# Four transformer layers on one core: own LayerNorm chains for the first four token tiles, a one-step norm, another token order, later loads of the feed-forward weights

## The chip, the cores and the metric

The kernel runs on one core of one Trainium2 chip. A core has five engines with queues of their own: PE (TensorE, matrix products), ACT (ScalarE), DVE (VectorE), POOL (GpSimd) and SP (SyncE, which here only issues DMAs). They meet through semaphores alone; each executes its queue in order. The metric is the device time of one execution in microseconds (us), as the median of several runs. Beside the times stands one profiled execution, from which all the durations come.

## What is computed

x has 2048 tokens of 512 elements, bf16. Two layers alternate, A, B, A, B, each with a LayerNorm ahead and a residual sum behind:

```python
x = x + A(layernorm(x))      # linear attention, 32 heads of 16
x = x + B(layernorm(x))      # relu(x @ w1) @ w2, 512 -> 1376 -> 512

# A:  q, k, v = x @ wqkv;  phi(t) = where(t > 0, t + 1, exp(t)) + 1e-6
kv  = einsum("bhsd,bhse->bhde", phi(k), v)      # a sum over all tokens
z   = einsum("bhsd->bhd", phi(k))
o   = einsum("bhqd,bhde->bhqe", phi(q), kv) / (einsum("bhqd,bhd->bhq", phi(q), z) + 1e-6)
return o @ wo
```

Tokens meet only in the sums kv and z, and these do not depend on the order of the tokens.

## The kernel before

**Tiles and stages.** The tokens are cut into 16 tiles of 128 (one token per partition) and 4 chunks of 4 tiles. For each tile: statistics, norm (`xn`), transposition (`Tb`, features on partitions). Layer A then takes, in its pass `p1` over chunks, the K projection of each tile (`a_k`, four matmuls of 512 columns) and the Q projection of each chunk (`a_q`, four groups of four matmuls). Each projection is evacuated from PSUM by `phi_evac` (L489): two passes of ACT (linear, exp) and two of DVE. `a_z` and `a_g` sum z and G = xn^T phi(K); V is never projected for each token, since kv = G Wv is made once from G (`a_kv`), masked to the heads (KVT, L569), multiplied by wo (`a_m`) and copied to `Mf` (L576). `a_fin` applies Mf to the scaled phi(Q). Between these, `a_den` makes the denominators and `a_pqs` (matmuls of `rdc`, "rdx") scales phi(Q) by them. `bar` is that middle stage. Layer B is `b_h` (w1, relu) and `b_out` (w2, residual).

**What sets the order.** The kernel first lists all operations with what they read and write, with a duration assumed for each, and `_list_schedule` (L118) then fixes every engine's queue: the earliest start wins within a window of the listed operations. Operations given as `add_flex` may go to one of several engines, by the assumed durations. PSUM has 8 banks, handed out in the same pass. So a changed duration or dependence reorders queues far behind it.

**First loads.** SP issues, in this order (L364 to L384): tile 0 of x (`ld_x0a`), tiles 1 to 3, the K and the Q columns of wqkv, chunks 1, 2 and 3 of x, the V columns, wo, w1, and w2 in two parts. Tile n holds the tokens 128 n to 128 n + 127, so that in DRAM a partition's row of one tile is 1 KB, and the four rows of a chunk lie 128 KB apart.

**First statistics.** `ln_stats_first` (L426) is bn_stats and bn_aggr on DVE, giving mean and variance (`mv`). Then `veps` (DVE), the power -0.5 on POOL (`rstd`), `nbias` = -mean * rstd (DVE), and the norm xn = x * rstd + nbias. Tile 0 has a chain of its own (L713 to L725), tiles 1 to 3 share one (L726 to L737). Chunks 0 and 1 are transposed on PE (`transpose_pe`, L472, evacuated by ACT or DVE, L485 and L486), chunks 2 and 3 by DMA transposes (L467) on SP. The first of these waits for all the weight loads (`ALL_LOADS`, L386, L751).

**Warm-up.** 16 matmuls of zeros (L399) run on PE while the first loads come.

Of the kernel before, what the change touches and what calls it, by code (L numbers as in the profile page):

```python
# [7 lines left out]
ALU = alu_op_type.AluOpType  # L8
ACTF = mybir.ActivationFunctionType
# [22 lines left out]
C_DVE_NORM_BF = 325.0  # L32
C_POOL_POW = 1000.0
C_POOL_NORM = 900.0
C_SP_ISSUE = 60.0
# [209 lines left out]
def build_kernel(nc, A_x, A_wqkv, A_wo, B_w1, B_w2, out, n_layers_pairs=2, K_STT=0, Q_STT=0, A_PE_CHUNKS=1, windows=None,  # L245
                 WARM=16, SPLIT0=True, TAIL_SPLIT=True, LAST_HALVES=True, FIRST_PE_CHUNKS=2,
                 flex_strict=True, flex_bias_dve=0.0):
# [18 lines left out]
    with es:  # L266
# [39 lines left out]
        nhalf = sb("nhalf", [128, 4], F32)  # L306
        veps0 = sb("veps0", [128, 1], F32)
        rstd0 = sb("rstd0", [128, 1], F32)
        nbias0 = sb("nbias0", [128, 1], F32)
        wrm = sb("wrm", [128, 512], BF16)  # L310
# [52 lines left out]

        x_v = A_x[0].rearrange("(n p) d -> p n d", p=128)  # L364
        out_v = out[0].rearrange("(n p) d -> p n d", p=128)
        def ld_x(t, lo=0):
            dma(lambda e, t=t: e.dma_start(xin[:, 4 * t + lo:4 * t + 4, :], x_v[:, 4 * t + lo:4 * t + 4, :]),
                [], [("xin", i) for i in range(4 * t + lo, 4 * t + 4)], 1500.0 * (4 - lo) / 4.0, "ld_x%d" % t)
        dma(lambda e: e.dma_start(xin[:, 0, :], x_v[:, 0, :]), [], [("xin", 0)], 450.0, "ld_x0a")
        wq_v = A_wqkv.rearrange("(c p) n -> p c n", p=128)  # L370
        ld_x(0, 1)
        dma(lambda e: e.dma_start(wqkv[:, :, D:2 * D], wq_v[:, :, D:2 * D]), [], [("wk",)], 1500.0, "ld_wk")  # L372
        dma(lambda e: e.dma_start(wqkv[:, :, 0:D], wq_v[:, :, 0:D]), [], [("wq",)], 1500.0, "ld_wq")  # L373
        for t in range(1, NCH):
# [4 lines left out]

        dma(lambda e: e.dma_start(w1[:], B_w1.rearrange("(c p) n -> p c n", p=128)), [], [("w1",)], 4000.0, "ld_w1")  # L380
        dma(lambda e: e.dma_start(w2[:, 0:nfull, :], B_w2[0:nfull * 128, :].rearrange("(c p) n -> p c n", p=128)),
            [], [("w2a",)], 3800.0, "ld_w2a")
        if FLAST < 128:
            dma(lambda e: e.dma_start(w2[0:FLAST, NFC - 1, :], B_w2[nfull * 128:DFF, :]), [], [("w2b",)], 600.0, "ld_w2b")  # L384
        W2KEYS = [("w2a",), ("w2b",)] if FLAST < 128 else [("w2a",)]
        ALL_LOADS = [("wk",), ("wv",), ("wq",), ("wo",), ("w1",)] + W2KEYS  # L386

# [5 lines left out]
        if WARM > 0:  # L393
            wt = alloc_bank()

            def _warm(e):
                last = None
                for k in range(WARM):
                    last = e.matmul(psv[:, wt, :], wrm[:, 0:128], wrm[:, :], start=True, stop=True)  # L399
                return last  # L400
            g.add(PE, _warm, [("wrm",)], [("ps", wt)], WARM * 400.0, name="warm")
        g.add(POOL, lambda e: e.memset(onesf[:], 1.0), [], [("onesf",)], 200, name="ms_ones")
# [22 lines left out]

        def ln_stats_first(i):  # L426
            g.add(DVE, lambda e: e.bn_stats(bst[:, i, :], xin[:, i, :]), [("xin", i)], [("bst", i)], C_DVE_BNST, name="bnst%d" % i)  # L427
            g.add(DVE, lambda e: e.bn_aggr(mv[:, i, :], bst[:, i, :]), [("bst", i)], [("mean", i), ("var", i)], C_DVE_SMALL, name="bnag%d" % i)
# [269 lines left out]
        def store_chunk(t):  # L698
            if t == NCH - 1 and TAIL_SPLIT:
# [9 lines left out]
                [("xin", i) for i in range(4 * t, 4 * t + 4)] + [("T", i) for i in range(NT)], [("out", t)], 1500.0, "st%d" % t)  # L709

        def ln_first(t):
            if t == 0 and SPLIT0:
                ln_stats_first(0)  # L713
                g.add(DVE, lambda e: e.tensor_scalar(veps0[:, :], mv[:, 0, 1:2], 0.0, EPS, ALU.max, ALU.add),
                      [("var", 0)], [("veps0",)], C_DVE_SMALL, name="veps0a")
                g.add(POOL, lambda e: e.tensor_tensor(rstd0[:, :], veps0[:, :], nhalf[:, 0:1], ALU.pow),
                      [("veps0",), ("nhalf",)], [("rstd0",)], C_POOL_POW, name="rstd0a")
                g.add(DVE, lambda e: e.scalar_tensor_tensor(nbias0[:, :], mv[:, 0, 0:1], -1.0, rstd0[:, :], ALU.mult, ALU.mult),
                      [("mean", 0), ("rstd0",)], [("nbias0",)], C_DVE_SMALL, name="nbias0a")
                g.add_flex([(DVE, lambda e: e.tensor_scalar(xn[:, 0, :], xin[:, 0, :], rstd0[:, 0:1], nbias0[:, 0:1], ALU.mult, ALU.add),  # L720
                             C_DVE_NORM_BF),
                            (ACT, lambda e: e.activation(xn[:, 0, :], xin[:, 0, :], ACTF.Identity, scale=rstd0[:, 0:1],
                                                         bias=nbias0[:, 0:1]), C_ACT_SB_AP)],
                           [("xin", 0), ("rstd0",), ("nbias0",)], [("xn", 0)], name="norm0a")
                transpose_pe(0)  # L725
                for i in range(1, 4):  # L726
                    ln_stats_first(i)
                sl = slice(1, 4)
                g.add(DVE, lambda e: e.tensor_scalar(veps[:, sl], mv[:, sl, 1], 0.0, EPS, ALU.max, ALU.add),
                      [("var", i) for i in range(1, 4)], [("veps", 0)], C_DVE_SMALL, name="veps0b")  # L730
                g.add(POOL, lambda e: e.tensor_tensor(rstd[:, sl], veps[:, sl], nhalf[:, 0:3], ALU.pow),
                      [("veps", 0), ("nhalf",)], [("rstd", 0)], C_POOL_POW, name="rstd0b")
                g.add(DVE, lambda e: e.scalar_tensor_tensor(nbias[:, sl], mv[:, sl, 0], -1.0, rstd[:, sl], ALU.mult, ALU.mult),
                      [("mean", i) for i in range(1, 4)] + [("rstd", 0)], [("nbias", 0)], C_DVE_SMALL, name="nbias0b")
                for i in range(1, 4):
                    ln_norm(i, True)
                    transpose_pe(i)  # L737
                return
            for i in range(4 * t, 4 * t + 4):
                ln_stats_first(i)  # L740
            ln_chunk(t, True)
            for i in range(4 * t, 4 * t + 4):
                ln_norm(i, True)
                if t < FIRST_PE_CHUNKS:
                    transpose_pe(i)
            if t >= FIRST_PE_CHUNKS:
                tr_dma(t)
# [18 lines left out]
        def layer_steps(layer):  # L766
# [3 lines left out]
            if layer % 2 == 0:  # L770
# [4 lines left out]
                def p1(t):  # L775
                    if first_layer and t + 1 < NCH:
                        ln_first(t + 1)
                    for i in range(4 * t, 4 * t + 4):
                        a_k(i)
# [194 lines left out]
```

## Time and profile before

| what | value |
|---|---|
| median of 3 runs | 294.8 us (293.8 to 294.86) |
| the profiled execution | 295.03 us, of which span 293.3 us |
| PE busy | 283.8 us (97%) |
| ACT busy | 170.3 us (58%) |
| DVE busy | 158.1 us (54%) |
| POOL busy | 33.1 us (11%) |
| DMA, mean over the span | 57 GB/s |
| granted TensorE clock | 1.0 |

The span runs from the first to the last instruction of the program; what is left of the execution's time lies around it. The page of the profile has the busy time of each engine, the span cut into 40 slices (a digit for each, in tenths), the chain of work that ended last, the costliest groups of instructions and the DMA issues. The chain is followed back from the last instruction, at each step to what released it; where it names a DMA or another engine, the engine that waited stood still. In the timeline each line has start, duration, engine, source line, operation, what is written and read, and in brackets how long the engine was idle before and who released it. PEld is the load of matmul weights, and SPq is SP issuing a DMA.

### The profile page before, as it was taken

Reading aid. Unit: us, or ns where it says so; the run is one execution under the profiler, and the core shown is the slowest. Engines: PE = TensorE matmul, PEld = TensorE weight load, DVE = VectorE, ACT = ScalarE, POOL = GpSimd, SP = SyncE. Lnnn points to the kernel's source line nnn. Section 1 sums busy time; section 2 is a strip of 40 time slices with the busy share of each in tenths; the row PEclk is TensorE's granted clock in tenths of the full one; section 3 lists DMA queues with packets and bytes.
Section 4 is the critical chain, followed back from the end, with each engine's and each line's share of the span. In section 5 each row is a group of like instructions: output and inputs, shape, how many; then the busy total and the mean of one; then the engine's idle time right before and its main releaser. Section 6 shows DMA issues by size and latency. Waiting matters only on the chain.

```text
span 293.3 us, 4232 instructions
## 1 busy us (share of the span) xinstructions
PE 283.8 (97%) x1610; PEld 133.5 (46%) x1636; DVE 158.1 (54%) x443; ACT 170.3 (58%) x351; POOL 33.1 (11%) x43
## 2 busy tenths in 40 slices
PE   7699999989999999999999999999999999999996
PEld 3345444434454454454444444444445445454444
DVE  5699774999720293361454748928973037020122
ACT  2798496687765365397434999248786505407000
POOL 4012100002410040020020300000241002000000
PEclk9999999999999999999999999999999999999999
DMA  7991330000260016031003300000026003303022
GB/s 221 356 370 41 64 54 0 2 0 0 52 130 0 2 35 126 1 71 21 0 2 72 70 4 0 0 2 0 1 58 124 0 2 91 72 2 89 0 74 72
DMA packets 37796, 16.72 MB, mean 57 GB/s; under 512 B 29616, under 2 KB 37264, under 8 KB 37776
## 3 DMA queue, kind: packets, MB, share of 16 engines
q1 hardware_dynamic: 37776, 16.45, 22.8%
q8 instruction: 13, 0.21, 0.3%
q14 instruction: 7, 0.06, 0.1%
HBM read 7.01 MB, written 2.10 MB: 31 GB/s over the span
## 4 chain that ended last, share of the span: by engine, by line
PE 88%; DVE 6%; DMA 3%; ACT 2%; issue 1%; SPq 1%
PE ps L510 87%; DMA xin<-in_A_x_dram 3%; DVE big L606 2%; DVE xn L459 1%; DVE xres L521 1%; ACT Mf L576 1%; ACT big L493 1%; PE ps L481 0%; DVE bst L427 0%; DVE big L503 0%; DVE emscr L497 0%; ACT sqscr L527 0%; SPq L373 0%; ACT escr L495 0%; SPq L372 0%
## 5 line engine op out<-in xcount | busy, mean ns | idle before, releaser
L510 PE MATMUL ps<-w,big 128*128 128x512 bf16 (+3 forms) x355 | 76.0, 372 | 0.4
L510 PE MATMUL ps<-Tb,w 128*128 128x512 bf16 x320 | 70.4, 379 | 0.0
L510 PEld LDWEIGHTS ps<-w,big 128*128 128x128 bf16 (+1 forms) x363 | 35.3, 98 | 40.4
L527 ACT ACTIVATE sqscr<-xres 128x512 bf16<-128x512 f32 x48 | 30.0, 628 | 40.1 <-DVE xres L521 39.6
L655 ACT ACTIVATE big<-ps 128x512 bf16<-128x512 f32 x70 | 41.6, 598 | 17.9 <-PE ps L510 17.9
L510 PEld LDWEIGHTS ps<-Tb,w 128*128 128x128 bf16 x320 | 30.8, 98 | 35.9
L493 ACT ACTIVATE big<-ps 128x512 bf16<-128x512 f32 x64 | 41.2, 648 | 9.0 <-PE ps L510 8.8
L521 DVE SCALAR_TENSOR_TENSOR xres<-ps,xres 128x512 f32<-128x512 f32 x32 | 21.9, 689 | 38.2 <-PE ps L510 38.0
L495 ACT ACTIVATE escr<-ps 128x512 bf16<-128x512 f32 x64 | 41.6, 667 | 0.4 <-DVE emscr L497 0.4
L447 POOL TENSOR_TENSOR rstd<-veps,nhalf 128x4 f32<-128x4 f32 x15 | 16.1, 1070 | 204.5 <-DVE veps L445 183.3
L518 DVE TENSOR_TENSOR xin<-ps,xres 128x512 bf16<-128x512 f32 x15 | 10.4, 692 | 46.6 <-PE ps L510 46.6
L510 PE MATMUL ps<-wqkv,Tb 128*128 128x512 bf16 x122 | 28.6, 379 | 2.7 <-DVE Tb L486 1.2
L510 PE MATMUL ps<-Tb,wqkv 128*128 128x512 bf16 x128 | 30.6, 379 | 0.0
L510 PE MATMUL ps<-Mf,big 128*128 128x512 bf16 x122 | 29.0, 380 | 1.3 <-ACT Mf L576 0.8
L510 PE MATMUL ps<-big,xn 128*128 128x512 bf16 x124 | 29.7, 379 | 0.3
L497 DVE TENSOR_SCALAR emscr<-escr 128x512 bf16<-128x512 bf16 x64 | 18.4, 296 | 18.5 <-ACT escr L495 18.4
L503 DVE TENSOR_TENSOR big<-big,emscr 128x512 bf16<-128x512 bf16 x64 | 26.4, 421 | 1.2
L606 DVE TENSOR_TENSOR big<-big,ps 128x512 bf16<-128x512 bf16 x32 | 19.9, 680 | 1.3 <-PE ps L510 1.3
L510 PEld LDWEIGHTS ps<-wqkv,Tb 128*128 128x128 bf16 x128 | 12.1, 98 | 17.2 <-DVE Tb L486 1.7
L510 PEld LDWEIGHTS ps<-Mf,big 128*128 128x128 bf16 x128 | 11.9, 98 | 16.2 <-ACT Mf L576 1.3
L510 PEld LDWEIGHTS ps<-big,xn 128*128 128x128 bf16 x128 | 11.5, 97 | 13.1 <-issue 1.5
L510 PEld LDWEIGHTS ps<-Tb,wqkv 128*128 128x128 bf16 x128 | 11.5, 97 | 12.3 <-DVE big L606 0.4
(74 smaller groups left out, 196.2 us busy)
## 6 DMA issues: line engine op xcount, KB each, us to landing
wqkv<-in_A_wqkv_dram SPq DMA_DIRECT2D x3, 512.0 KB, 7.1
xin<-in_A_x_dram SPq DMA_DIRECT2D x3, 512.0 KB, 9.1
out_dram<-xin SPq DMA_DIRECT2D x3, 512.0 KB, 2.9
w<-in_B_w_dram SPq DMA_DIRECT2D x1, 1376.0 KB, 11.0
w<-in_B_w_dram SPq DMA_DIRECT2D x1, 1280.0 KB, 12.8
wo<-in_A_wo_dram SPq DMA_DIRECT2D x1, 512.0 KB, 9.4
xin<-in_A_x_dram SPq DMA_DIRECT2D x1, 384.0 KB, 3.2
out_dram<-xin SPq DMA_DIRECT2D x1, 256.0 KB, 2.1
```

What stands on the lines that cost most here:

```text
L447: g.add(POOL, lambda e: e.tensor_tensor(rstd[:, sl], veps[:, sl], nhalf[:, 0:4], ALU.pow), [("veps", t), ("nhalf",)], [("rstd", t)], C_POO ...
L459: (DVE, lambda e: e.tensor_scalar(xn[:, i, :], src, rstd[:, i:i + 1], nbias[:, i:i + 1], ALU.mult, ALU.add), C_DVE_NORM_BF if first else 4 ...
L493: g.add(ACT, lambda e: e.activation(dst_ap, psv[:, b, :], ACTF.Identity, bias=1.0 + 1e-6, scale=1.0), [("ps", b)], [dst_key], C_ACT_PSUM, ...
L495: g.add(ACT, lambda e: e.activation(escr[:, s, :], psv[:, b, :], ACTF.Exp), [("ps", b)], [("escr", s)], C_ACT_EXP, name=name + "_exp")
L497: g.add(DVE, lambda e: e.tensor_scalar(emscr[:, s, :], escr[:, s, :], 1.0, 1e-6, ALU.min, ALU.add), [("escr", s)], [("emscr", s)], C_DVE_B ...
L503: g.add(DVE, lambda e: e.tensor_tensor(dst_ap, dst_ap, emscr[:, s, :], ALU.max), [dst_key, ("emscr", s)], [dst_key], 340.0, name=name + "_ ...
L510: last = e.matmul(o, l, r, start=st, stop=sp, skip_group_check=skip)
L518: g.add(DVE, lambda e: e.tensor_tensor(xin[:, i, :], psv[:, b, :], src, ALU.add), [("ps", b), skey], [("xin", i)], C_DVE_PSUM, name="resid ...
L521: g.add(DVE, lambda e: e.scalar_tensor_tensor(xres[:, i, :], psv[:, b, :], 0.0, src, ALU.add, ALU.add, accum_out=s1[:, i:i + 1]), [("ps", ...
L527: g.add(ACT, lambda e: e.activation(sqscr[:, q, :], xres[:, i, :], ACTF.Square, accum_out=s2[:, i:i + 1]), [("xres", i)], [("sqscr", q), ( ...
L606: g.add(DVE, lambda e, j=j, u=u: e.tensor_tensor(unit_ap(u), unit_ap(u), psv[:, bs[j], :], ALU.mult), [("ps", bs[j]), ("big", u)], [("big" ...
L655: g.add_flex([(ACT, lambda e, M=M, b=b, u=u: e.activation(unit_ap(u, M), psv[0:M, b, :], ACTF.Relu), C_ACT_PSUM), (DVE, lambda e, M=M, b=b ...
```

## The change

- Each of tiles 0, 1, 2 gets its own chain: bn_stats, bn_aggr, `veps`, a one-column power on POOL, norm. The statistics of tile 2 wait until tile 0 is normed and tile 1's `veps` is done. Tile 3's mean and mean square are summed by two passes of ACT, and its variance and `veps` are made by POOL.
- The norm of these four tiles is one step, (x - mean) * rstd, on DVE alone; `nbias` and the choice between ACT and DVE are gone for them.
- Tokens are dealt the other way: partition p holds the tokens 16 p to 16 p + 15, one for each tile, in the input and the output. A partition's row of a chunk is 4 KB on end, with 16 KB from partition to partition.
- w1 and w2 are loaded after the DMA transposes of chunks 2 and 3 (`ld_ff`), and the first DMA transpose no longer waits for them.
- The warm-up has 13 matmuls instead of 16. Some assumed durations are changed, of x and weight loads and of the warm-up.

```diff
-                 WARM=16, SPLIT0=True, ...
+                 WARM=13, SPLIT0=True, ...
-        x_v = A_x[0].rearrange("(n p) d -> p n d", p=128)
-        out_v = out[0].rearrange("(n p) d -> p n d", p=128)
+        x_v = A_x[0].rearrange("(p n) d -> p n d", p=128)
+        out_v = out[0].rearrange("(p n) d -> p n d", p=128)
...
+        def ld_ff():
+            after = [("T", i) for i in range(4 * FIRST_PE_CHUNKS, NT)]
+            dma(... w1 ..., after, [("w1",)], 4000.0, "ld_w1")
+            dma(... w2 ..., after, [("w2a",)], 3800.0, "ld_w2a")
+            if FLAST < 128:
+                dma(... w2 ..., after, [("w2b",)], 600.0, "ld_w2b")
-        ALL_LOADS = [("wk",), ("wv",), ("wq",), ("wo",), ("w1",)] + W2KEYS
+        ALL_LOADS = [("wk",), ("wv",), ("wq",), ("wo",)]
...
+        def ln_own(i):
+            mu = mv[:, i, 0:1] if i < 3 else mean[:, i:i + 1]
+            g.add(POOL, lambda e: e.tensor_tensor(rstd[:, i:i + 1], veps[:, i:i + 1], nhalf[:, 0:1], ALU.pow),
+                  [("veps1", i), ("nhalf",)], [("rstd1", i)], C_POOL_POW1, name="rstd_%d" % i)
+            g.add(DVE, lambda e: e.tensor_scalar(xn[:, i, :], xin[:, i, :], mu, rstd[:, i:i + 1], ALU.subtract, ALU.mult),
+                  [("xin", i), ("mean", i), ("rstd1", i)], [("xn", i)], C_DVE_NORM_BF, name="norm%d" % i)
+            transpose_pe(i)
...
             if t == 0 and SPLIT0:
+                for i in range(3):
+                    ln_stats_first(i, [("xn", 0), ("veps1", 1)] if i == 2 else [])
+                    g.add(DVE, ... veps[:, i:i + 1] <- mv[:, i, 1:2] ..., C_DVE_TINY, name="veps_%d" % i)
+                    ln_own(i)
+                g.add(ACT, lambda e: e.activation(sqscr[:, 0, :], xin[:, 3, :], ACTF.Identity, scale=INV_D, accum_out=mean[:, 3:4]), ...)
+                g.add(ACT, lambda e: e.activation(sqscr[:, 1, :], xin[:, 3, :], ACTF.Square, scale=INV_D ** 0.5, accum_out=s2[:, 3:4]), ...)
+                g.add(POOL, ... nm2[:, 3:4] <- mean * mean ..., name="nm2_3")
+                g.add(POOL, ... var[:, 3:4] <- s2 - nm2 ..., name="var_3")
+                g.add(POOL, ... veps[:, 3:4] <- max(var, 0) + EPS ..., name="veps_3")
+                ln_own(3)
                 return
...
                     if first_layer and t + 1 < NCH:
                         ln_first(t + 1)
+                        if t + 2 == NCH:
+                            ld_ff()
```

## The prediction

> **What bounds the kernel now.** First the page's busy line and its 40 slices.
>
> ```profile
> span 293.3 us, 4232 instructions
> PE 283.8 (97%) x1610; PEld 133.5 (46%) x1636; DVE 158.1 (54%) x443; ACT 170.3 (58%) x351; POOL 33.1 (11%) x43
> ...
> PE   7699999989999999999999999999999999999996
> ```
>
> TensorE (PE) is the bound: 283.8 of 293.3 us, and its digit is below 9 only in the first two slices, once near 60 us and in the last. Only there can this change gain or lose. Of 9.5 us not busy, 1.25 stand ahead of the first warm-up matmul and about 2 behind the last matmul. So I read the chain that ended last, in order of time, for what the first slices wait on.
>
> ```profile
> 2.78 8.10 DMA xin<-in_A_x_dram
> 10.90 1.29 DVE bst L427 x2
> 12.19 0.33 DVE Tb L486
> 12.57 4.49 PE ps L510 x20
> 17.06 1.32 PE ps L481 x16
> ...
> 58.21 1.97 ACT Mf L576 x4
> 60.22 6.67 PE ps L510 x32
> ```
>
> Up to 10.9 us the end hangs on the load of token tiles 4 to 7 (I call it x1): issued at 2.78, landed 8.1 us later. DVE has tile 4's statistics queued ahead of a PSUM copy (L486) that two K projections need, so tiles of the first chunk wait for a load of the second. The timeline of PE shows where it stands still:
>
> ```profile
> 6.98 0.40 PE L481 MATMUL ps<-ident,xn 128*128 128x128 bf16 x4 [0.28 <-DVE xn L720]
> 8.07 1.04 PE L510 MATMUL ps<-wqkv,Tb 128*128 128x512 bf16 x4 [0.63 <-ACT Tb L485]
> 8.94 0.83 PE L481 MATMUL ps<-ident,xn 128*128 128x128 bf16 x12
> 10.28 1.04 PE L510 MATMUL ps<-wqkv,Tb 128*128 128x512 bf16 x4 [0.51 <-ACT Tb L485]
> 12.57 1.90 PE L510 MATMUL ps<-wqkv,Tb 128*128 128x512 bf16 x8 [1.25 <-DVE Tb L486]
> 14.30 2.75 PE L510 MATMUL ps<-Tb,wqkv 128*128 128x512 bf16 x12
> 17.01 1.36 PE L481 MATMUL ps<-ident,xn 128*128 128x128 bf16 x16
> 18.21 1.03 PE L510 MATMUL ps<-Tb,wqkv 128*128 128x512 bf16 x4
> 19.29 3.40 PE L510 MATMUL ps<-wqkv,Tb 128*128 128x512 bf16 x15
> ```
>
> A group of 4 matmuls of 512 columns occupies PE for 0.864 us (12.57 to 14.30 for two). The last row has 15 records of 16, so the K projection of tile 4 began one matmul earlier, at 19.29 - 0.22 = 19.07. I measure the change at this point, because PE has hardly a gap from there to 57 us.
>
> **First chunk, until its Q projection ends.** The load of tile 0 landed at 2.97, that of tiles 1 to 3 (x0) at 4.44, the K weights at 6.05, the Q weights at 9.37 (issue plus time to landing).
> 1. Tile 0: statistics and rsqrt end at 4.74 as now. Removed is nbias; the norm no longer stands behind three bn_stats but behind one: 4.46 + 0.62 = 5.08, plus 0.38 = 5.46 (now it starts at 6.54). The warm-up loses 3 matmuls of 0.216 us and ends at 6.70 - 0.65 = 6.05. So the transposes start at 6.05 instead of 6.98, bound by the warm-up with 0.6 us to spare. ACT copies 0.44 us later (6.98 to 7.42 now) for 0.60: K projection 0 starts at 7.14, not 8.07; its weights are there.
> 2. Tiles 1 and 2 each get an own chain: bn_aggr, veps, a one-column pow on POOL (0.56 in the row of tile 0; the three-column one took 0.86), norm (0.41, next start after 0.33). Tile 3's sums go to ACT, idle from 2.54 to 7.42: one pass with accumulator by rows of 0.62 to 0.81 plus 0.19, the square 0.62 + 0.19, done by 6.3. No row shows a one-column multiply or subtract on POOL; below stands its memset of one column, 0.10, above the one-column pow, 0.56. Three such operations precede the pow of tiles 1 or 3, so 0.3 to 1.7 us of POOL time; I take 0.2 each, since they have no power in them. Norms 1, 2, 3 then end near 7.2, 8.4 and 9.0, the last one 9.4 at the upper price.
> 3. PE: K projection 0 until 8.00, transposes 1 to 3 until about 9.2. ACT: one evacuation of K 0 at 8.2, then the copies of tiles 1, 2, 3, each 0.48 to 0.55 after the last, from 8.7. K projections 1, 2, 3 start at 9.35, 10.2, 11.1 and end at 11.95 (14.30 now). All 16 matmuls of Q 0 follow without a wait and end at 15.4; now twelve of them end at 16.89 and four come after 18.21.
>
> **Second chunk: when x1 lands.** From x1's landing to the first transpose DVE now needs 6.11 us (10.90 to 17.01). In the changed order I count four bn_stats (2.37), four bn_aggr (0.33), two emscr (0.40), veps (0.15 + 0.06), the 128x4 pow (1.31 here), nbias and a product (0.40), norm (0.41), with hand-overs 5.55. So the landing decides, and for that I read the issues of the DMA queue:
>
> ```profile
> 2.78 2.00 SPq L367 DMA_DIRECT2D xin<-in_A_x_dram  x3
> 4.82 2.62 SPq L376 DMA_DIRECT2D wqkv<-in_A_wqkv_dram  x1
> 7.49 1.82 SPq L377 DMA_DIRECT2D wo<-in_A_wo_dram  x1
> ```
>
> An issue takes 0.4 to 0.5 us until three x loads of 512 rows are queued; then 2.62 and 1.82. In the same time the Q weights land 3.32 us after the K weights, though later loads of that size follow each other by 1.50 (10.88, 12.38, 13.88). The change makes the rows of x four times as long, 128 a load instead of 512. Best case: the 1.8 us of excess are a full queue and go; x1 lands at 6.05 + 1.5 + 1.5 = 9.05. Worst from these rows: nothing changes, 10.88. The longest rows here (2752 bytes, w1) came 3.54 us after wo for 1376 KB, 398 GB/s against 350: some 0.25 us of the two x loads. I take 10.0, midway, since both facts stand in the trace and their link does not. Then the first transpose is at 10.0 + 5.55 = 15.55 and PE idles 0.15; ACT's copy (0.42 later, 0.60) puts K projection 4 at 16.62. The lead is 19.07 - 16.62 = **2.45 us**. At x1 = 9.05 PE is the bound, 15.4, and the lead 2.5; at 10.88 it is 16.43, 17.50 and 1.6.
>
> A rule speaks against the new layout: the Trainium skill, "DMA: Bandwidth & Descriptors", section "Latency and other measured facts", says that row pitches of large powers of two slow HBM copies, 207 GB/s at a pitch of 512 KiB. The new pitch per partition is 16 KiB, which that table lacks; every load here ran near 350 GB/s. By the rule's figure, as an estimate, x0 and x1 together would take about 2 us longer and the lead would be about 0.4.
>
> **From there to the end.** PE has no gap over 0.1 us from 19.29 to 57 in this trace and ACT sat idle 4.15 us before 33.89 and 2.65 before 48.51, so ACT can follow a PE that is 2.5 us ahead: 43 ACT passes at a pitch of 0.48 remain, 21 us from 17.6. The order changes in one place that costs: at the end of the first attention layer. Now one Q group (0.86) stands between the four matmuls with wo and the first use of Mf, and covers most of the four Mf copies; still PE waits 0.79 at 60.22. In the new order this Q group is ahead of them, and four G matmuls have gone before the first rdx. From rdx (51.22 now) the start of the first use is +9.00 now. New: wo matmuls at +6.35 (KVT of DVE, +6.3, decides), three more ACT passes are done by +6.65, first Mf copy +6.75, three pitches of 0.48 and 0.60 more give +8.8; but rdx itself comes 0.86 later, behind the moved G. Loss 9.7 - 9.0 = **0.7 us**; 0.3 if KVT's products find no bank wait, 0.9 if ACT is one pass late. Behind that the order on all engines is the same to the end, and PE is the chain but for two short DVE stretches near 67 to 71 and 159 to 166, which move with it.
>
> w1 and w2 (three issues) now stand on SP behind both DMA transposes, and wait for their landing, 39.40 now. Landing takes 1.4 + 8 us at 350 GB/s, done by 50; first use is 73.49, and the next thing behind them on SP is at 74.95. Cover 23 us: cost nothing. The output's longer rows touch no store of the last 1.5 us, whose rows are 512 bytes as before: nothing, within 0.2.
>
> **Sum.** 2.45 - 0.7 = 1.75 us gained. The profiled execution took 295.03 (span 293.3 and 1.73 around it): 293.28 by it. That execution lies 0.23 above the median 294.8; against the median I get 293.05, given as **293.1**.
>
> **Rivals.**
> - *x1 lands about as now*, 10.5 to 10.9, or the Mf wait grows to 0.9: gain 1.6 - 0.7 = 0.9, from 0.4 to 1.3, time 293.9. For it: the same queue, the same bytes ahead. Chance 0.26.
> - *x1 early and the Mf wait covered*: 2.5 - 0.3 = 2.2, up to 2.9 if the transposes of chunk 1 also tighten; 292.4. Chance 0.17.
> - *Lead given back later*: between 60 and 72 DVE is busy 11.37 of 12 us. If its order there makes PE wait for PSUM, the gain is gone; 294.7, within 0.4. For it: the chain's DVE pieces at 66.9 to 71.7; against: they start after the same matmuls. Chance 0.07.
> - *Slower: strided x loads.* Tile 0 now comes as rows of 1 KB at 16 KB pitch, as do x0 and x1. If they run at under half the 350 GB/s, the 1 MB takes over 3 us more, x1 lands past 13.2, the transposes start at 18.8 and K projection 4 at 19.8, 0.75 late; with the Mf loss 296.3. Decides from x1 = 11.8 on (no lead left after Mf). Against: the slowest early slice still ran at 273 GB/s. Chance 0.06.
> - The forecast itself, gain 1.3 to 2.3: 0.44.
>
> **How the numbers follow.** About 0.5% (1.5 us) is what can be told from no change. Three quarters of the forecast (0.33) and the second rival (0.17) lie beyond it: faster 0.50. The rest of the forecast (0.11), the first and the third rival (0.33): 0.44 within. Slower 0.06. The range takes the first three rivals' ends: 291.9 (2.9 gained) to 294.9.
>
> **What would show it.** First transposes at 6.05, K projection 0 near 7.1, tile 0's norm at 5.1 behind one bn_stats; x1's landing near 10 with issues of SP back at 0.4 to 0.5 us; K projection 4 near 16.6; the wait on Mf about 1.3 instead of 0.79 us; all later stages of equal length. I am wrong if x1 lands past 11, if POOL's small operations take over 0.6 us each, if the 13 warm-up matmuls no longer reach the short pitch, or if PE gets new gaps between 20 and 57 us.

## The result, and the profile after

| | before | after |
|---|---|---|
| median of 20 runs each, same chip | 294.34 us (293.73 to 295.02) | 293.71 us (293.02 to 294.05) |
| the profiled execution | 295.03, span 293.3 | 293.31, span 291.5 |

The ratio is 0.9977, with a 95% interval of 0.9967 to 0.9986: 0.63 us faster by the medians, where 1.7 were forecast. The two profiled executions lie 1.7 us apart, and the forecast was worked out on the first of them. So the sum held between these two executions and not between the kernels. The first is 0.7 above the median of its kernel, the second 0.4 below that of its own. The rest of this document is about that difference.

The busy line and the 40 slices of the kernel after:

```profile
PE 284.4 (98%) x1633; PEld 133.4 (46%) x1633; DVE 157.1 (54%) x440; ACT 170.6 (59%) x355; POOL 36.0 (12%) x48
...
PE   7999999899999999999999999999999999999996
```

PE is the bound as before. The digit below 9 in the middle has moved one slice forward and is still there: the stall at Mf stays.

The chain of waits of the kernel after (start, duration, what), in order of time:

```profile
1.25 3.93 DMA xin<-in_A_x_dram
5.20 0.69 DVE bst L428
...
7.88 1.09 POOL rstd L714 x2
8.99 0.42 DVE xn L716
...
9.86 6.04 PE ps L511 x28
...
56.49 1.97 ACT Mf L577 x4
```

The head of the chain is no longer the load of tiles 4 to 7 (issued at 2.73 here) but that of tiles 1 to 3, issued at 1.25. It leads through the statistics of the first chunk to two powers on POOL (1.09 us) and the norm of tile 3 at 8.99. From there PE is the chain, up to the Mf copies at 56.49. The second chunk's load does not appear at all.

PE's timeline over the same stretch as in the prediction, and at the end of the first attention layer:

```profile
6.26 0.40 PE L482 MATMUL ps<-ident,xn 128*128 128x128 bf16 x4 [0.20 <-DVE xn L716]
7.35 1.04 PE L511 MATMUL ps<-wqkv,Tb 128*128 128x512 bf16 x4 [0.63 <-ACT Tb L486]
...
9.69 2.75 PE L511 MATMUL ps<-wqkv,Tb 128*128 128x512 bf16 x12
12.28 3.62 PE L511 MATMUL ps<-Tb,wqkv 128*128 128x512 bf16 x16
15.73 0.84 PE L482 MATMUL ps<-ident,xn 128*128 128x128 bf16 x12
...
16.94 3.61 PE L511 MATMUL ps<-wqkv,Tb 128*128 128x512 bf16 x16
...
58.51 2.76 PE L511 MATMUL ps<-Mf,big 128*128 128x512 bf16 x12 [1.22 <-ACT Mf L577]
```

The 16 matmuls of Q 0 follow K projections 1 to 3 without a gap, and the transposes of chunk 1 follow Q 0 without a gap. The waits of 0.51 and 1.25 us of before are gone. K projection 4 starts at 16.94 (all 16 records are there), which is 2.13 us ahead of the 19.07 in the profile of before. At the first use of Mf the wait is 1.22 instead of 0.79, with 0.18 more inside the matmuls with wo; there the lead is 60.22 - 58.51 = 1.71.

### The profile page after: what moved, and what is told of

The parts are those of the page before. It is cut to its first block, busy times and chain, and to the rows that moved or that the text cites. A ratio compares the mean times of both kernels' runs of the same rounds, so it can differ in the third digit from the quotient of the medians.

```text
span 291.5 us, 4263 instructions
## 1 busy us (share of the span) xinstructions
PE 284.4 (98%) x1633; PEld 133.4 (46%) x1633; DVE 157.1 (54%) x440; ACT 170.6 (59%) x355; POOL 36.0 (12%) x48
## 4 chain that ended last, share of the span: by engine, by line
PE 90%; DVE 4%; ACT 2%; DMA 1%; issue 0%; POOL 0%; SPq 0%
PE ps L511 89%; DMA xin<-in_A_x_dram 1%; ACT big L494 1%; DVE big L607 1%; DVE xn L460 1%; PE ps L482 1%; DVE xres L522 1%; ACT Mf L577 1%; ACT escr L496 1%; DVE bst L428 0%; DVE big L504 0%; DVE emscr L498 0%; POOL rstd L714 0%; DVE xn L716 0%; ACT sqscr L528 0%
## 5 line engine op out<-in xcount | busy, mean ns | idle before, releaser
L511 PE MATMUL ps<-w,big 128*128 128x512 bf16 (+2 forms) x363 | 77.3, 372 | 0.0
L448 POOL TENSOR_TENSOR rstd<-veps,nhalf 128x4 f32<-128x4 f32 x15 | 17.3, 1153 | 200.4 <-DVE veps L446 181.7
L511 PE MATMUL ps<-Mf,big 128*128 128x512 bf16 x128 | 29.7, 380 | 1.3 <-ACT Mf L577 1.2
L511 PE MATMUL ps<-big,xn 128*128 128x512 bf16 x128 | 30.3, 379 | 0.0
L607 DVE TENSOR_TENSOR big<-big,ps 128x512 bf16<-128x512 bf16 x32 | 19.9, 681 | 1.5 <-PE ps L511 1.3
L511 PEld LDWEIGHTS ps<-wqkv,Tb 128*128 128x128 bf16 x128 | 12.2, 98 | 15.4 <-ACT Tb L486 0.8
```

What stands on the lines that cost most here:

```text
L511: last = e.matmul(o, l, r, start=st, stop=sp, skip_group_check=skip)
L607: g.add(DVE, lambda e, j=j, u=u: e.tensor_tensor(unit_ap(u), unit_ap(u), psv[:, bs[j], :], ALU.mult), [("ps", bs[j]), ("big", u)], [("big" ...
```

## The experiments

Kernels marked "from before" or "from after" are those kernels with the edit shown. Every ratio is against the kernel before on the same chip. Lines of PE named below as "K projection 4" are corrected by 0.22 us where the record of its first matmul is missing.

**1. The kernel before, once more.** No edit.

> The kernel before, unchanged, for its spread and a second profile. Question: the two profiles differ by 1.8 us of span, the two medians by 0.63 us. Theory A (the profiled execution of before was one with a late x load, landing 10.88): executions spread over more than 1 us, the low ones near 293.8, and a profile of a low one shows chunk 1 of x landing before 10 and the copy ahead of K projection 2 earlier than 12.1 by as much. Rival B (the gain of 1.8 us is in every execution and something around the span eats it): any profile of before has a span near 293.3 and x landing near 10.9.

Measured: 294.29 us (293.71 to 294.51), ratio 0.9998 [0.9987, 1.0009]. Its profiled execution took 293.79, span 292.1, and PE's timeline after K projection 0 reads:

```profile
9.27 0.83 PE L481 MATMUL ps<-ident,xn 128*128 128x128 bf16 x12
10.61 2.76 PE L510 MATMUL ps<-wqkv,Tb 128*128 128x512 bf16 x12 [0.51 <-ACT Tb L485]
```

The first statistics of chunk 1 on DVE:

```profile
9.68 1.29 DVE L427 BATCH_NORM_STATS2 bst<-xin 128x6 f32<-128x512 bf16 x2 [0.45 <-DMA xin<-in_A_x_dram]
```

The 1.25 us wait in front of the last two K projections, which the prediction made the centre of its sum, is not there: K projections 1 to 3 run as one group of 12. In this execution x1 landed at 9.66, not at 10.88, and the span is 1.2 shorter. Theory A holds, though these runs spread over 0.8 us and not over 1. The profile that the prediction read was one of the same kernel with a late x load; the clock does not explain the difference, since the warm-up took 5.46 us there and 5.51 here. K projection 4 starts at 17.85, the first use of Mf at 59.00. Against this execution the kernel after leads by 0.91, then 0.49, and by 0.57 at the end, close to the 0.63 of the medians. This is a comparison of two single executions, 0.5 and 0.4 us below the medians of their runs. In the profiles of runs 4, 5, 6 and 9, whose queues begin as in the kernel after, K projection 4 starts at 17.20 to 17.41 and not at 16.94, so that the nearness to 0.63 is in part luck.

**2. The token layout alone** (from before).

```diff
-        x_v = A_x[0].rearrange("(n p) d -> p n d", p=128)
-        out_v = out[0].rearrange("(n p) d -> p n d", p=128)
+        x_v = A_x[0].rearrange("(p n) d -> p n d", p=128)
+        out_v = out[0].rearrange("(p n) d -> p n d", p=128)
```

> The kernel before with the new token order alone; all queues keep their order. Theory A (four times fewer rows of x unblock the load queue): K weights near 6.9, Q weights near 8.4 and chunk 1 of x near 9.7 as in the changed kernel, issues of SP at 0.4 to 0.6 us; the copy behind tile 4's statistics comes 1.2 us earlier than in the first profile, so span near 292.2 and the spread narrower; about 0.5 us below the median of before. Rival C (the 16 KB pitch slows the loads): tile 0 lands 0.4 and K weights 0.8 us later and the time is 0.3 to 0.8 us over that of before.

Measured: 294.11 (293.63 to 294.21), ratio 0.9997 [0.9988, 1.0006]: no difference that can be told. Two issues of SP (start, duration):

```profile
4.49 0.74 SPq L376 DMA_DIRECT2D wqkv<-in_A_wqkv_dram  x1
5.27 0.51 SPq L377 DMA_DIRECT2D wo<-in_A_wo_dram  x1
```

The issues of 2.62 and 1.82 us that the prediction showed are now 0.74 and 0.51, so with the long rows SP is done sooner. But x1 landed at 9.84, no earlier than in run 1 (9.66), while the first loads came later: tiles 1 to 3 at 5.08 instead of 4.77, the K weights at 7.05 instead of 6.18. Long issues and a late landing are two things: in run 1 the same two issues took 1.88 and 1.30 us, and x1 was on time.

**3. The old layout in the kernel after** (from after; the edit of run 2 in reverse).

> The changed kernel with the old token order; all queues keep their order. Theory A: tiles 1 to 3 land at 4.4 instead of 5.2 and K weights at 6.05, but chunk 1 of x late in part of the executions (10.9 instead of 9.65): first transposes at 6.05, the ones of chunk 1 at 16.4 instead of 15.73 in those; time from 0.3 below to 0.7 above the changed kernel, with a spread over 1 us. Rival C: 0.5 to 0.8 us faster than the changed kernel in all executions.

Measured: 293.69 (292.98 to 296.04), ratio 0.9990 [0.9972, 1.0008]; profiled 293.24. The median is that of the kernel after, so nothing here speaks for the layout as the source of the gain; the interval alone tells run 3 neither from the kernel after nor from the kernel before. The runs spread over 3.1 us, those of the kernel after over 1.0 us, but half of that is one execution: 296.04, with a mean granted clock of 0.994, where the other eleven have 0.999 or 1.0 and end at 294.55. In the profile tiles 1 to 3 landed at 4.50 and the K weights at 5.97, about 0.7 and 0.9 ahead of the kernel after. K projection 1 started 0.41 earlier, at 9.28, and K projection 4 still at 16.93: the transposes of chunk 1 (15.53) now had to wait for its norms, 5.89 us after x1 landed at 9.64.

**4. w1 and w2 issued early again** (from after).

```diff
-        def ld_ff():
-            after = [("T", i) for i in range(4 * FIRST_PE_CHUNKS, NT)]
-            dma(... w1 ..., after, [("w1",)], 4000.0, "ld_w1")
+        dma(... w1 ..., [], [("w1",)], 4000.0, "ld_w1")
...
-        ALL_LOADS = [("wk",), ("wv",), ("wq",), ("wo",)]
+        ALL_LOADS = [("wk",), ("wv",), ("wq",), ("wo",), ("w1",)] + W2KEYS
```

> The changed kernel with w1 and w2 issued right behind wo again, and the first DMA transpose waiting for them; only SP's order differs. Prediction: nothing, within 0.2 us of the changed kernel, since wo lands at 15.1 and w1, w2 by 24 in either order before the first transpose is due at 26.9. Rival D (the loads of w1 and w2 press on the queue): Q weights and chunk 1 of x land 1 us later or more, the time is 0.5 us or more over that of the changed kernel.

Measured: 293.64 (293.24 to 293.99), ratio 0.9982 [0.9972, 0.9993]; profiled 293.64. w1 landed at 19.12 instead of 45.21, and nothing followed from it. The late loads show neither a cost nor a gain.

**5. One Q group held back for the Mf copies** (from after). The last of the four Q groups of chunk 3 is made to wait for KVT, so that it stands between the matmuls with wo and the first use of Mf, as in the kernel before. `also` names what a group waits for besides its own operands.

```diff
-        def a_q(t, js=(0, 1, 2, 3)):
+        def a_q(t, js=(0, 1, 2, 3), also=()):
...
-                    a_q(NCH - 1)
+                    if first_layer:
+                        a_q(NCH - 1, (0, 1, 2))
+                        a_q(NCH - 1, (3,), also=[("KVT",)])
+                    else:
+                        a_q(NCH - 1)
```

> The changed kernel with the last Q group of the first layer made to wait for KVT, so that it stands between the wo matmuls and the first use of Mf as in the kernel before. Theory (0.6 us of the lead are given back at the Mf copies, 1.22 + 0.18 us of waiting against 0.80): wait on Mf 0.8 or less, first use of Mf near 58.0 instead of 58.5, time 0.3 to 0.6 us below the changed kernel, about 293.2. Rival (DVE is the bound behind it, from 60 to 72 us): the wait shrinks but the first matmul of layer B stays near 71.65 and the time stays at 293.7.

Measured: 293.49 (293.37 to 293.74), ratio 0.9977 [0.9968, 0.9987]; profiled 293.51.

```profile
56.54 0.81 PE L511 MATMUL ps<-wo,KVT 128*128 128x512 bf16 x3 [1.03 <-ACT escr L496]
...
58.86 2.76 PE L511 MATMUL ps<-Mf,big 128*128 128x512 bf16 x12 [0.65 <-ACT Mf L577]
```

The wait for Mf falls from 1.22 to 0.65, and a new one of 1.03 opens ahead of the matmuls with wo: the work that covered that place was moved away from it. The wait changed its place. The ratio is that of the kernel after: nothing was gained, and the theory's 0.3 to 0.6 us did not come. So the four copies are not the whole of the loss. KVT is late as well: it ended at 56.26, 0.16 ahead of the evacuation on ACT that released the matmuls with wo.

**6. Two Q groups held back** (from after; the same edit with groups 2 and 3).

> The same with the last two Q groups behind the wo matmuls; the planner then also gives one of the four Mf copies to DVE. Theory: the copies are covered fully, wait on Mf under 0.3 us, 0.6 to 1.0 us below the changed kernel, about 292.9. Rival (DVE is the bound behind it): no more than e5; DVE's extra copy makes the first residuals 0.7 us late and layer B begins no earlier than in the changed kernel.

Measured: 298.14 (297.75 to 299.20), ratio 1.0138 [1.0117, 1.0159]. Neither theory nor rival foresaw the loss. The planner put KVT (57.81) behind twelve products of DVE instead of eight, and PE stood still for 4.19 us, up to 58.95. What that cost on top shows in the busy times by stretch (PE busy first after the length and the comma; the number after POOL's is the granted clock):

```profile
55.00:59.00 4.00, 0.05 (x1) 0.18 (x3) 4.00 (x9) 0.28 (x1) 0.00 (x0) 0.71 0.00 0
59.00:63.00 4.00, 4.00 (x10) 1.46 (x10) 1.25 (x3) 2.50 (x5) 0.00 (x0) 0.50 0.01 4
```

From 59 to 63 PE is busy without a break at a clock of 0.50, and only 10 matmuls start in 4 us; from 64 on the clock is 1.00 again. The long idle time was paid for a second time after it had ended. The clock row of the pages of before and after, whose waits reach 1.25 us, shows no such fall.

**7 and 8. x1 issued ahead of the Q weights** (7 from before, 8 from after).

```diff
+        ld_x(1)
         dma(... wqkv[:, :, 0:D] ..., "ld_wq")
-        for t in range(1, NCH):
+        for t in range(2, NCH):
```

> The kernel before with chunk 1 of x issued ahead of the Q weights and nothing else edited; the planner then reorders, and in its new order no Q group covers the Mf copies. Theory (x1's landing sets when the kernel before runs steadily): x1 lands near 8 instead of 9.7 to 10.9, the copy of tile 3 no longer stands behind it, projections of K 2 start near 11, K projection 4 near 17 instead of 17.9 to 19.1; about 0.5 us given back at Mf (wait 1.2 instead of 0.8); time 293.3 to 293.8, as fast as the changed kernel without any of its chains. Rival (the own chains carry the gain): 294.1 or more.

> The changed kernel with chunk 1 of x issued ahead of the Q weights. Theory (PE, not x1, bounds the changed kernel from 9.5 us on, with x1's chain 0.2 us behind the Q projection's end): K projection 4 between 16.6 and 17.0, the time within 0.3 us of the changed kernel, unless the planner's new order moves the Mf wait. Rival (x1 bounds it still): 0.8 us or more below.

Measured for 7: 296.35 (294.48 to 296.98), ratio 1.0058 [1.0035, 1.0081]: slower, although x1 landed at 8.49. PE's timeline and DVE's, of the kernel of run 7:

```profile
11.03 1.46 PE L482 MATMUL ps<-ident,xn 128*128 128x128 bf16 x12 [2.07 <-DVE xn L460]
12.29 3.67 PE L511 MATMUL ps<-wqkv,Tb 128*128 128x512 bf16 x12
```

```profile
8.51 0.69 DVE L428 BATCH_NORM_STATS2 bst<-xin 128x6 f32<-128x512 bf16 x1 [1.65 <-DMA xin<-in_A_x_dram]
...
9.92 0.14 DVE L734 SCALAR_TENSOR_TENSOR nbias<-mv,rstd 128x3 f32<-128x3 f32 x1
```

The planner, told of an earlier load, put the first bn_stats of chunk 1 ahead of the `nbias` of tiles 1 to 3. DVE stood 1.65 us in front of it, and all that is queued behind it, the norms of the first chunk among them, waited for a load of the second. It is the fault that the prediction had seen in the profile of before, with a larger wait. After its 2.07 us of idle time PE ran K projections 1 to 3 in 3.67 us instead of 2.75, at a granted clock of 0.50 between 11 and 14 us. So run 7 does not tell what an early x1 alone is worth. The eleven executions fall in two groups: six took 296.35 to 296.98, at a mean granted clock of 0.993 or 0.994, and five took 294.48 to 295.21 at 1.00. Most of the loss thus goes with the fall of the clock; without it the order still costs some 0.6 us. The theory missed, and the rival's "294.1 or more" was met for another reason than the rival's.

Measured for 8: 294.03 (293.59 to 294.42), ratio 0.9998 [0.9987, 1.0008]. x1 landed at 8.29, 1.4 us earlier than in the kernel after, and K projection 4 started at 17.68, 0.74 later: the planner's order brought waits of 0.81 and 0.73 us at 9.39 and 11.60. An earlier x1 gained nothing here either, but here too the order moved with it, and the theory (K projection 4 between 16.6 and 17.0, the time within 0.3 us) missed.

**9 and 10. KVT made earlier** (from after). `a_pqs` scales phi(Q) of one chunk by its denominators: four matmuls of `rdc` and four products on DVE (L607). In the first attention layer those of chunks 1 and 2 are listed behind `a_m`, the matmuls with wo (run 9), or behind the last Q projection (run 10).

```diff
-                            if n in (3, 5, 7):
+                            if n in ((3,) if first_layer else (3, 5, 7)):
                                 a_pqs((n - 3) // 2)
...
                     a_m(KB)
+                    if first_layer:
+                        a_pqs(1)
+                        a_pqs(2)
                     a_q(NCH - 1)
```

What the two expectations call "products of K and V" are these products of `a_pqs`.

> The kernel after, with the products of K and V of chunks 2 and 3 in the first attention layer listed behind the last K and V projection, so that VectorE makes the masked copy KVT after four of these products instead of after eight. TensorE's work stays the same; its order at the end of the first attention layer becomes: last K and V projection, four Q projections, the four matmuls with wo, eight Q projections, first use of Mf. Theory (what is lost at Mf is the wait for KVT and the four copies behind it): the two waits there, 0.18 and 1.22 us in the kernel after, fall below 0.3 us together, the second attention layer's first matmul of hr starts at 70.5 to 71.0 instead of 71.65, and the median is 292.9 to 293.2. Rival (VectorE is the bound in the stretch from 58 to 72, so that what is won at Mf is waited for later): hr starts at 71.4 or later and the median is 293.5 to 293.9.

> The same idea with another listing: the products of K and V of chunks 2 and 3 are listed behind the Q projections of the last chunk, and the matmuls with wo stand behind four Q projections, with eight Q projections between them and the first use of Mf. Theory: as in the run before it, waits below 0.3 us together, median 292.9 to 293.2. Rival: median 293.5 to 293.9.

Measured for 9: **292.80** (292.48 to 293.12), ratio 0.9951 [0.9933, 0.9968], 1.3 us below the kernel before (294.10 on this chip), better than the kernel after against its own before (0.9977 [0.9967, 0.9986]; the two intervals just meet). PE's timeline:

```profile
55.06 1.89 PE L511 MATMUL ps<-Tb,wqkv 128*128 128x512 bf16 x8
...
57.21 6.22 PE L511 MATMUL ps<-Mf,big 128*128 128x512 bf16 x28
...
69.55 1.90 PE L511 MATMUL ps<-Mf,big 128*128 128x512 bf16 x8 [0.93 <-DVE big L607]
```

Both waits at Mf (0.18 and 1.22 us) are gone: eight Q matmuls stand between wo and Mf, and KVT is at 53.10 on DVE instead of 55.16. A new wait of 0.93 opens at 69.55, for products of DVE, which is busy for all of the 8 us from 58 to 66. The theory holds for the place of the loss and its cause; the rival's bound, DVE, takes part of it back. The start of the second layer's first matmul, which the expectation named, is no measure, since the planner has put more of the Mf matmuls ahead of it. By a later mark (the third stage of w2 matmuls, 111.36 against 111.69) run 9 leads the kernel after by 0.33, and at the end by 0.35, though in this execution it was 0.47 behind at 51.8.

Measured for 10: 293.70 (293.26 to 294.03), ratio 0.9979 [0.9961, 0.9998], the rival's number. With this order the waits at Mf are gone too, but three come in their place (0.57 and 0.17 us for DVE's products at 59.83 and 61.37, 0.46 at 72.47), 1.20 for 1.40 us. The ratio is that of the kernel after.

**11 and 12. Sixteen warm-up matmuls** (from after). In run 11 the planner knew of the three more; in run 12 only the loop was lengthened, and the order of all queues stayed.

```diff
-                 WARM=13, ...
+                 WARM=16, ...
```

```diff
-                for k in range(WARM):
+                for k in range(WARM + 3):
```

> The kernel after with 16 warm-up matmuls instead of 14: the first transposes can start no earlier than about 6.7 us instead of 6.26. The planner moves a few instructions of the first two token chunks as well. Theory (in the kernel after, the start of K projections 1 to 3 is set by the chains of statistics on VectorE and GpSimd, which end at 9.0 to 9.4, and not by TensorE's warm-up): the median stays within 0.2 us of the kernel after, 293.5 to 293.9. Rival (TensorE's own work from the first transposes on sets the end): the added 0.45 us arrive at the end, 294.1 to 294.3.

> The kernel after with three more warm-up matmuls (16 as in the kernel before), the queues of all engines otherwise in exactly the order of the kernel after; in the run before it the planner had moved instructions as well, which is undone here. (In that run's expectation the kernel after was said to have 14 warm-up matmuls; it has 13.) In the kernel after the warm-up ended at 6.06 us, the first transposes started at 6.26, released by the norm of tile 0, and the transposes of tiles 2 and 3 at 8.94, released by their norms. Theory (what the run before it lost lies in the moved order, that is in its waits of 0.85 us at 11.75 and 0.39 at 33.0, and not in the three matmuls): the warm-up ends 0.65 us later, near 6.7, and the norms of tiles 2 and 3 still release the transposes near 9; K projections 1 to 3 start at most 0.2 us later than 9.69, and the median is 293.6 to 294.0. Rival (TensorE's own work from the warm-up on is the bound, so the cut from 16 to 13 is where the gain of the change comes from): the three matmuls arrive at the end in full, 0.65 us, and the median is 294.2 to 294.5, no better than the kernel before.

Measured for 11: 294.79 (294.34 to 295.07), ratio 1.0014 [0.9997, 1.0031]: later than theory and rival allowed. Measured for 12: 294.19 (293.65 to 294.54), ratio 0.9983 [0.9966, 0.9999]. Against the kernel before on their own chips the medians of the kernel after, run 12 and run 11 stand at -0.63, -0.23 and +0.69: 0.4 for the three matmuls and 0.9 for the moved order. By the intervals of the ratios run 12 can't be told from the kernel after. Its median lies between the theory's 294.0 and the rival's 294.2. The profile says why neither fits. The warm-up of the kernel after, and the warm-up and what follows it in run 12:

```profile
1.24 4.82 PE L400 MATMUL ps<-wrm 128*128 128x512 bf16 x13 [1.24 <-DVE wrm L393]
```

```profile
1.24 6.50 PE L400 MATMUL ps<-wrm 128*128 128x512 bf16 x16 [1.24 <-DVE wrm L393]
7.57 0.39 PE L482 MATMUL ps<-ident,xn 128*128 128x128 bf16 x4
...
10.86 2.76 PE L511 MATMUL ps<-wqkv,Tb 128*128 128x512 bf16 x12
```

```profile
8.05 0.22 DVE L425 COPY Esel<-ps 128x128 bf16<-128x128 bf16 x1 [0.85 <-PE ps L423]
```

Sixteen matmuls that start as in the kernel before took 6.50 us here and 5.46 there. They are spaced 0.43 us at first and 0.216 from some moment on, and that moment is not the same in every execution: it came at 5.0 us in the profiles of before and after and at 7.1 in run 12. The first transposes of run 12 start at 7.57 with no wait for a norm, so the warm-up was the bound. K projection 1 is 10.86 - 9.69 = 1.17 late, and the span 1.2 longer. Of the 1.68 us that the warm-up ended later (6.50 against 4.82 from the same start), some 0.65 are the three matmuls and 1.04 the later moment (6.50 against 5.46). The execution with the profile is the slowest of the twelve; the five fastest took 293.65 to 293.95. So the statistics do not cover a longer warm-up, as the theory had it. The line of DVE shows one reason: the copy to `Esel` waits for a matmul that follows the first transposes on PE, and it stands ahead of the norms of tiles 1 to 3, so that these come late as well (norm 3 ends at 10.33 instead of 9.41). The norm of tile 0 and the warm-up end so close together that either binds, by the execution: the first transposes wait for the norm in the profiles after, 4 and 9, and for no norm in those of runs 3, 5, 6, 10 and 12. Run 11 mixes all this with the planner's new order (waits of 0.85 us at 11.75 and 0.39 at 33.00) and decides nothing by itself.

## Why the prediction was right, and where it was not

| | forecast | profile before to profile after | run 1 to profile after |
|---|---|---|---|
| lead at K projection 4 | 2.45 | 2.13 | 0.91 |
| given back until Mf is used | 0.7 | 0.42 | 0.42 |
| at the end | 1.75 | 1.8 | 0.57 |

**The step that failed** is the sum's reference: "The profiled execution took 295.03 ... That execution lies 0.23 above the median 294.8; against the median I get 293.05." With it goes "Worst from these rows: nothing changes, 10.88" for the landing of x1. The 10.88 was that execution's own. With x1 at 9.66 (run 1) the 1.25 us wait, which the change was to remove, does not exist, and K projection 4 starts at 17.85 instead of 19.07. Of the 2.45 us, 1.22 are this. That the sum nevertheless met the two profiles, 1.75 against 1.8, is luck: the lead at K projection 4 came 0.32 short, and 0.28 less was given back at Mf. The three times shown at first (293.8, 294.8, 294.86) had one about 1 us below the others, and the later runs put the profiled execution 0.7 above a median of 294.34. The measured gain of 0.63 lies below the forecast's own 1.3 to 2.3. It lies in the 0.4 to 1.3 of the first rival (x1 as now, 293.9), which had nearly the right number from the wrong side: it took x1 to stay late in both kernels, and x1 came at 9.6 to 10.2 in every profile here with the loads in this order but the first one.

- *First chunk.* The forecast had the first transposes at 6.05, K projection 0 at 7.14, K projection 1 at 9.35, Q 0 done at 15.4. Measured: 6.26, 7.35, 9.69, 15.73. The order of events is as said. "The norm no longer stands behind three bn_stats but behind one" is right, but that one waits for tiles 1 to 3, which landed at 5.18 instead of 4.44 with the new layout, so norm 0 ran from 5.81 to 6.21 and bound instead of the warm-up. The prices on POOL were a little low: 0.26, 0.19 and 0.39 us for the three operations taken at 0.2 each, and 1.09 for two powers in a row; norm 3 ended at 9.41, the upper price named. One sign named for being wrong, that the 13 warm-up matmuls "no longer reach the short pitch", was met in the profiles of runs 5 and 10: the warm-up ended at 6.93 and 6.97 there, and at 6.06 in the kernel after.
- *Second chunk.* "So the landing decides" does not hold in the profile after: with x1 at 9.65 PE went from Q 0 to the transposes without a gap. PE decided, 0.33 late from the first chunk. x1's landing came inside the bounds given (9.05 to 10.88), 0.35 from the value taken, and cost nothing. But its chain was close behind: in run 3, with the first chunk 0.41 ahead, it did decide. It was longer than summed, 5.89 us there for 5.55, by about what the 128x4 power took more, 1.66 for 1.31.
- *Why x1 lands when it does.* The guess was that short issues mean an early landing. Run 2 has the short issues, and x1 at 9.84. The rule of the Trainium skill, "DMA: Bandwidth & Descriptors", section "Latency and other measured facts", that large power-of-two pitches slow a copy, agrees in sign with the first loads: tiles 1 to 3 landed at 4.44, 4.77 and 4.50 with the old layout (before, runs 1 and 3) and at 5.18 and 5.08 with the pitch of 16 KiB (after, run 2), the K weights behind them at 6.05, 6.18, 5.97 and at 6.85, 7.05. The estimate made from it, 2 us for both loads, was not borne out: x1 came at 9.65 and 9.84, no later than the 9.66 and 9.64 of runs 1 and 3. Pitch and row length changed together, so no run shows which of them delayed the first loads.
- *Mf.* The place, the cause and the sign are right, and the loss is 0.42 for 0.7. Wait 1.22 + 0.18 for "about 1.3". From rdx to the first use of Mf it took the forecast 8.8 us (49.71 to 58.51); rdx came 0.62 later by the moved work, and not 0.86. Run 9 shows that KVT, queued behind eight products on DVE, sets it, as "KVT of DVE, +6.3, decides" had it.
- *w1 and w2, the output, later stages.* Nothing, as said: run 4 for the loads; from Mf to the end the lead changes by 0.1.
- *Rivals.* Strided loads that make it slower: with the new layout tiles 1 to 3 came 0.3 to 1.1 us later and x1 at 8.3 to 10.2, not past the 11.8 from which that rival decides. The lead given back between 60 and 72: not in the kernel after, whose order leaves DVE just enough room; it came in run 9, where 0.93 us open at 69.55 once the loss at Mf is gone.

What gains the 0.63 us is thus the first chunk (own chains, one-step norms, the shorter warm-up), less the loss at Mf. Runs 2 and 4 show no gain from the layout or the late weights, and the median of run 3 agrees. How the gain divides can be read from the start of K projection 1, on single executions:

| profiles | K projection 1 starts | first transposes start |
|---|---|---|
| before, runs 1 and 2 | 5.84 to 5.85 us after the landing of tiles 1 to 3 | 2.54 us after that landing, behind the norm of tile 0 |
| after, runs 4 and 9 | 4.51 to 4.52 us after that landing | 1.08 to 1.09 us after it, behind the norm of tile 0 |
| runs 3, 5 and 12 (warm-up last) | 3.29 us after the first transposes | directly behind the warm-up |

Tile 0 has landed some 1.5 us or more before. Its norm still depends on the landing of tiles 1 to 3, because statistics of theirs stand ahead of it in the queue of DVE, three in the kernel before and one in the kernel after. The changed chains shorten the way from that landing to K projection 1 by 1.33 us. The later landing (5.18 against 4.77 in run 1) gives 0.41 back, which leaves 0.92, and K projection 4 leads by 0.91. The shorter warm-up keeps this path free. With 16 matmuls done at 6.75, as in run 1, the transposes could start at about 6.58 (in runs 3 and 12 they start 0.17 ahead of the end that the profile gives the warm-up), and by the last row K projection 1 at 9.87 instead of 9.69. That is an estimate of 0.2 us for the warm-up; in executions with a later moment it is more, and by the medians of run 12 it is 0.4, which its interval does not tell from nothing. No run separates the own chains from the one-step norms. That the spread of the kernel before comes from x1's landing is seen in two profiles only. The other executions have no trace, and the landing of tiles 1 to 3 (4.44 to 4.77 in the kernel before) and the warm-up (5.46 to 5.97 us for 16 matmuls in before, runs 1 and 2) scatter too.

## What to carry to other kernels

Before a sum is made on one profiled execution, ask whether its longest wait belongs to the kernel or to that execution: a wait behind a load is the first suspect, and a spread of the times as large as the expected gain is the sign. A wait that goes at one place comes back where the same queue is next late, so ask which instruction stands at the head of the queue behind it; here an edit that moved only cover (run 5) gained nothing, one that moved the late producer (run 9) gained about as much again as the whole change. With a planner that orders queues by assumed durations, lengthen or move a thing without telling it (run 12) as well as with (run 11); otherwise the new order is measured, and not the edit.

## What the runs showed of the hardware that was not expected

- PE's granted clock fell to 0.50 around an idle time of 2.07 us (run 7, for some 3.4 us) and in one of 4.19 us (run 6, for some 6.8 us), while waits up to 1.25 us in the kernels before and after left it at 1.00. In run 7 six of eleven executions show the fall, and they took 1.1 to 2.5 us longer than the other five.
- The moment at which matmuls at the start go from a spacing of 0.43 to 0.216 us varies between executions (5.0 in the kernel before, 7.1 in run 12), although all started at 1.24: 16 matmuls took 4.92 us in the profile of run 7, 5.46 in that of before and 6.50 in that of run 12. The granted clock reads 1.00 in these stretches, so the spacing shows it and the clock row does not.
- Rows of x four times as long (run 2 against run 1) shortened the issue of the three x loads on SP from 2.13 to 1.72 us together, and the two issues behind them from 1.88 and 1.30 to 0.74 and 0.51. They brought x1 and the loads ahead of it in no earlier, and chunks 2 and 3 of x up to wo at most 0.3 us earlier.
